# Attention scores from pairs of float16 products, with the softmax sums moved between engines

## The chip, the cores and the metric

The kernel runs on one core of one Trainium2 chip. The metric is the device time of one execution in microseconds (us). A core has TensorE (PE, matrix products), VectorE (DVE), ScalarE (ACT), GpSimd (POOL) and SyncE (SP, which here only issues transfers); each engine runs its own list of instructions in order, and waits for the others by semaphores.

## What is computed

Soft-capped attention (2 batches, 12 heads, 448 positions, head size 64) is followed by two feed-forward layers (768 to 2048 to 768, ReLU squared, then SiLU) over 896 tokens.

```python
def _attn_ref(q, k, v, cap) -> np.ndarray:
    scale = 1.0 / np.sqrt(q.shape[-1])
    scores = scale * np.matmul(q, k.transpose(0, 1, 3, 2))
    scores = cap * np.tanh(scores / cap)
    scores = scores - np.max(scores, axis=-1, keepdims=True)
    attn = np.exp(scores)
    attn = attn / (np.sum(attn, axis=-1, keepdims=True) + 1e-09)
    return np.matmul(attn, v).astype(np.float32)
...
    x = _moe_ref(x=x, **moe_kwargs)      # relu(x @ w_in) ** 2 @ w_out
    return _moe2_ref(x=x, **moe2_kwargs) # silu(x @ w_in) @ w_out
```

Inputs and output are float32.

## The kernel before

The 24 heads (of both batches) are 12 pairs; a pair fills the 128 partitions of one `qk` tile with the 64 rows of q (and of k) of two heads. Two pairs, `A` and `B`, make a "quad" m = 0 to 5. The 448 keys of a pair are three pieces of 128 (`A0`, `A1`, `A2`, `B0`, ...) and a rest of 64; the rests of both pairs share one block, `C`. So a quad has seven blocks in the order A0 A1 A2 C B0 B1 B2, and all six quads have 42.

`attention_bounded` walks over them in 21 groups of two blocks; h counts the groups. What is emitted in pass h, in this order, is what each engine then runs in order:

- `scores` (L636 on): TensorE multiplies k by q in float32 into one of two score tiles in PSUM, one product per head (two for `C`, one for each pair); ScalarE takes the tanh of it into an `e` tile (8 of them). A/B products use 64 rows by 128 columns of the array, `C` products 64 by 64.
- ScalarE takes the exp of both blocks (L746), in place. So ScalarE's list is tanh, tanh, exp, exp for each group.
- loads: `pr.load` puts the q and k of the next quad's pairs on SP's queue (L581, L582; six `qk` tiles), behind what is queued there already.
- VectorE copies finished attention sums `px` out of PSUM (L703), then `add` (L669 on; L675, L677) adds up the exponentials of each pair's blocks into `total`, the rest block `C` too (L681).
- `values` (L652 on): TensorE multiplies v by the exponentials of the group before.
- At a quad's end `add_up` (L683 on) sums `total` over its partitions with TensorE (four float32 products with ones); `evacuate_sums` (L705 on) copies the result with VectorE to `sm`, and SP gathers it to `st`; a pass later `invert` (L712 on) takes reciprocals on VectorE and SP writes them to `scratch` in memory, and then SP fetches them back, spread over partitions, as `rb`. `normalise` multiplies with them.
- `ws.load_to` and `ws.step` slip the first feed-forward weights in: loads on SP, and between passes 5 and 16 twelve steps, eight of them VectorE's (lines L367, L395 and L220: `u_0f`, `hl_0f` and so on).

Elsewhere a float32 weight or activation is handled as a high and a low float16 part, and a product of two such pairs as three float16 products (`ORDER`: high by high, high by low, low by high). The feed-forward layers (line L934) already work so; the attention before does not. `Watch` collects the sums of the low parts (`low_part`, L215 on) and decides at the end whether a general path must run instead.

After the last pass, TensorE sums the last pair's exponentials (`sump`, L698) and goes on to the first feed-forward products (`ha_0f`).

Of the kernel before, what the change touches and what calls it, by code (L numbers as in the profile page):

```python
# [26 lines left out]
def softcap_attention_relu2_silu(  # L27
# [26 lines left out]
    WT = KT * 128  # L54
    HALF = KT // 2 * 128
    NHR = 2
    AHEAD = 6
    NR = 7
    BENT = 1
# [5 lines left out]

    POWER = {"x0": 16, "a": 13, "b": 14, "ga": 22, "x1": 23, "c": 13, "d": 14, "gc": 24}
    LOWS, SAMPLES = 256, KT + 10
    LEAST = 256.0 * 128 * S  # L70
    ONE = 2.0 ** -POWER["x0"]
# [8 lines left out]
    def bank(name):  # L80
        return psum.tile([128, 512], F32, tag="p", bufs=4, name=name)
# [11 lines left out]

    cap = cap.rearrange("(a b) -> a b", a=1)
    capt = const.tile([128, 1], F32, tag="capt", name="capt")
    cap1 = const.tile([1, 2], F32, tag="cap1", name="cap1")
    nc.scalar.dma_start(cap1[:, :1], cap)
    nc.gpsimd.dma_start(capt, cap.to_broadcast([128, 1]))

# [12 lines left out]
    def tile_of(w, t):  # L112
        at = 2 + t * 128 * WT * 8
        return w.bitcast(I8)[at : at + 128 * WT * 8].rearrange("(p n) -> p n", p=128)

    COL2 = 0.1892
    PROD, UNIT = 9 * COL2, 12 * COL2
    PLAIN = (("a", 0), ("a", 2))
# [453 lines left out]
    class Pairs:  # L572
# [1 line left out]


        def __init__(self, pool, tag):
            self.pool, self.tag, self.qk, self.vt, self.vc = pool, tag, {}, {}, {}

        def load(self, i):
            t = self.pool.tile([128, 2, S], F32, tag="qk", bufs=6, name=f"qk{i}{self.tag}")  # L580
            nc.sync.dma_start(t[:, 0], q[i])  # L581
            nc.sync.dma_start(t[:, 1], k[i])  # L582
            self.qk[i] = t

        def load_v(self, i):
            m, b = divmod(i, 2)
# [15 lines left out]
    def attention_bounded(att, spool, ws, x0):  # L602
# [15 lines left out]
        nc.vector.reciprocal(cap1[:, 1:], cap1[:, :1])  # L618
        nc.vector.tensor_scalar(cap1[:, 1:], cap1[:, 1:], SCALE, None, op0=ALU.mult)
        scale_s, scale_c = nc.scalar.alloc_register("scale_s"), nc.scalar.alloc_register("scale_c")  # L620
        nc.scalar.reg_load(scale_s, cap1[:, 1:].bitcast(I32))
# [5 lines left out]
        NQ = NP2 // 2  # L627
        blocks = [(m, x) for m in range(NQ) for x in ("A0", "A1", "A2", "C", "B0", "B1", "B2")]

        def pair_of(m, x):  # L630
            return 2 * m + "AB".index(x[0])

        def head(j):
            return slice(64 * j, 64 * j + 64)

        def scores(m, x):  # L636
            sp = bank2(spool, f"s{m}_{x}")
            for j in range(2):
                for b in range(2) if x == "C" else (None,):
                    qk = pr.qk[pair_of(m, x) if b is None else 2 * m + b]  # L640
                    c = 3 if b is not None else int(x[1])
                    nc.tensor.matmul(  # L642
                        sp[:, j, :S] if b is None else sp[head(b), j, :S],
                        lhsT=qk[head(j), 1, 128 * c : min(128 * c + 128, S)],
                        rhs=qk[head(j), 0],
                        start=True,
                        stop=True,
                    )
            t = ex[m, x] = att.tile([128, 2, S], F32, tag="e", bufs=8, name=f"e{m}_{x}")
            nc.scalar.activation(t, sp[:, :, :S], AF.Tanh, scale=scale_s)  # L650

        def values(m, x):  # L652
            for i in (2 * m, 2 * m + 1) if x == "C" else (pair_of(m, x),):
                if i not in px:
                    px[i] = bank(f"px{i}")
            e = ex[m, x]
            for b in range(2) if x == "C" else (None,):
                for j in range(2):
                    i = pair_of(m, x) if b is None else 2 * m + b
                    v_m = pr.vt[i]  # L660
                    nc.tensor.matmul(  # L661
                        px[i][head(j), :S],
                        lhsT=v_m[:, 3 * j + int(x[1])] if b is None else pr.vc[m][head(b), j],
                        rhs=e[:, j] if b is None else e[head(b), j],
                        start=x == "A0" or b == 1,
                        stop=x == "B2" or b == 0,
                    )

        def add(m, x):  # L669
            e, i = ex[m, x], None if x == "C" else pair_of(m, x)  # L670
            if i == NP2 - 1:
                return
            if x in ("A1", "B1"):
                t = total[i] = att.tile([128, 2, S], F32, tag=f"total{x[0]}", bufs=2, name=f"total{i}")
                nc.vector.tensor_tensor(t, ex[m, x[0] + "0"], e, op=ALU.add)  # L675
            if x in ("A2", "B2"):
                nc.vector.tensor_tensor(total[i], total[i], e, op=ALU.add)  # L677
            if x in ("C", "B1"):
                b = int(x == "B1")
                t = total[2 * m + b][head(b)]  # L680
                nc.vector.tensor_tensor(t, t, ex[m, "C"][head(b)], op=ALU.add)  # L681

        def add_up(m):  # L683

            s = sums[m] = bank(f"sum{m}")
            for b in range(2):
                for j in range(2):
                    at = 32 * (2 * b + j)
                    nc.tensor.matmul(  # L689
                        s[at : at + 32, :S], lhsT=one[:, :32], rhs=total[2 * m + b][:, j], start=True, stop=True  # L690
                    )

        def add_up_pair(i, t, start=True, stop=True, part=slice(0, 128)):
# [44 lines left out]
        todo, last = [], 2 * NQ - 2  # L738
# [124 lines left out]


    NEXT = {"a": "b", "c": "d"}
    ORDER = ((0, 0), (0, 1), (1, 0))

    def at(x):

# [861 lines left out]
```

## Time and profile before

| | before |
|---|---|
| median of 2 runs | 491.35 us (491.1 to 491.6) |
| profiled execution, its own time | 491.04 us |
| its span, first to last instruction | 489.1 us |
| TensorE busy | 481.5 us (98%) |
| VectorE busy | 433.2 us (89%) |
| ScalarE busy | 383.5 us (78%) |
| GpSimd busy | 33.2 us (7%) |
| granted TensorE clock | 0.998 |

The attention takes the first 87 us of the span and the feed-forward layers the rest. A line of a timeline gives the start and the length in us, engine, source line, operation, tiles (buffer numbers left out) and, in brackets, how long the engine had idled and for whom. In the chain of the work that ended last each piece stands with its start and length. "x8" counts records; a float32 product leaves two of them.

### The profile page before, as it was taken

The page shows a single profiled execution, that of the slowest core. Times are in us where ns is not written, and L with a number is a line of the kernel's source. Part 1 is how long each engine was busy: PE and PEld are TensorE (multiplying, and loading weights), DVE is VectorE, ACT ScalarE, POOL GpSimd, SP SyncE. Part 2 cuts the span into 40 slices and gives each one's busy share as a digit, 9 for nine tenths or more (in the row PEclk, how much of TensorE's full clock was granted, in tenths as well). Part 3 has the DMA queues.
Part 4 walks back from the last instruction along what each step waited for, and adds up shares of the span by engine and source line. Part 5 has one row for each costly group of instructions (what it writes and reads, how often), then busy time and mean ns, then how long its engine had stood idle before and what let it go on. Part 6 is the DMA issues. An engine that isn't in the chain of part 4 may idle for free.

```text
span 489.1 us, 7199 instructions
## 1 busy us (share of the span) xinstructions
PE 481.5 (98%) x2554; PEld 232.7 (48%) x2554; DVE 433.2 (89%) x810; ACT 383.5 (78%) x625; POOL 33.2 (7%) x35
## 2 busy tenths in 40 slices
PE   8999999999999999999999999999999999999995
PEld 4323333455555555555555555555555555545552
DVE  0779998997899999988799999999878999999983
ACT  5999996899989944999988879989868688792100
POOL 1001555300000000000000000000000000000000
PEclk9999999999999999999999999999999999999999
DMA  7847461243645123335573443222577953129024
GB/s 248 283 136 187 163 198 40 82 142 127 216 158 187 49 81 129 131 129 194 193 259 116 144 146 113 72 84 103 183 260 242 314 228 86 45 85 365 2 77 157
DMA packets 25843, 75.28 MB, mean 154 GB/s; under 512 B 3270, under 2 KB 17606, under 8 KB 25798
## 3 DMA queue, kind: packets, MB, share of 16 engines
q1 hardware_dynamic: 25620, 74.50, 45.9%
q8 instruction: 22, 0.36, 0.3%
q10 hardware_dynamic: 146, 0.23, 0.1%
q14 instruction: 23, 0.19, 0.1%
q0 software_dynamic: 32, 0.00, 0.0%
HBM read 66.39 MB, written 8.29 MB: 153 GB/s over the span
## 4 chain that ended last, share of the span: by engine, by line
PE 86%; DVE 9%; DMA 1%; issue 1%; ACT 1%; DVEq 0%; ACTq 0%
PE px L661 7%; PE p_6df L934 4%; PE p_4df L934 4%; PE p_0df L934 4%; PE p_2bf L934 4%; PE s_B L642 3%; PE s_A L642 3%; PE ha_0f L934 3%; PE yb_3f L934 3%; PE yb_0f L934 3%; PE yb_5f L934 3%; PE yb_4f L934 3%; PE yb_2f L934 3%; PE ha_1f L934 3%; PE yb_1f L934 3%; PE p_2df L934 2%
## 5 line engine op out<-in xcount | busy, mean ns | idle before, releaser
L650 ACT ACTIVATE e_A<-s_A 128x896 f32<-128x896 f32 x18 | 15.9, 919 | 4.1 <-PE s_A L642 3.9
L650 ACT ACTIVATE e_B<-s_B 128x896 f32<-128x896 f32 x18 | 15.9, 917 | 4.0 <-PE s_B L642 3.7
L746 ACT ACTIVATE e_A<-e_A 128x896 f32<-128x896 f32 x18 | 16.5, 955 | 0.0
L746 ACT ACTIVATE e_B<-e_B 128x896 f32<-128x896 f32 x18 | 16.5, 953 | 0.0
L1459 DVE SCALAR_TENSOR_TENSOR yf<-p_6df,yf 128x448 f32<-128x448 f32 x15 | 9.2, 623 | 5.1 <-PE p_6df L934 5.1
L681 DVE TENSOR_TENSOR total<-total,e_C 64x896 f32<-64x896 f32 x11 | 12.9, 1174 | 0.4
L884 DVE TENSOR_TENSOR yaf<-p_2bf,yaf 128x448 f32<-128x448 f32 x15 | 9.3, 621 | 0.7 <-PE p_2bf L934 0.5
L362 POOL CAST zerosf<-raw_wb_7f 128x768 f16<-128x768 bf16 x1 | 1.1, 1055 | 127.0 <-DVE u_33f L367 127.0
L1459 DVE SCALAR_TENSOR_TENSOR yf<-p_4df,yf 128x448 f32<-128x448 f32 x15 | 9.2, 620 | 0.3 <-PE p_4df L934 0.2
L677 DVE TENSOR_TENSOR total<-total,e_A 128x896 f32<-128x896 f32 x6 | 8.2, 1359 | 0.3
L220 DVE SCALAR_TENSOR_TENSOR x1f<-yaf,x1f 128x448 f16<-128x448 f32 x12 | 7.4, 619 | 0.8 <-ACT x1f L873 0.8
L675 DVE TENSOR_TENSOR total<-e_A,e_A 128x896 f32<-128x896 f32 x6 | 6.8, 1130 | 1.1 <-ACT e_A L746 1.1
L884 DVE TENSOR_TENSOR yaf<-yaf 128x448 f32<-128x448 f32 x12 | 7.3, 620 | 0.1
L873 ACT ACTIVATE x1f<-yaf 128x448 f16<-128x448 f32 x12 | 6.7, 565 | 0.1
L675 DVE TENSOR_TENSOR total<-e_B,e_B 128x896 f32<-128x896 f32 x5 | 6.5, 1294 | 0.0
L759 DVE TENSOR_SCALAR gcap<-gcap 128x1 f32<-128x1 f32 x1 | 0.2, 154 | 6.8 <-ACT gcap L758 6.8
L364 ACT ACTIVATE zerosf<-raw_wa13f 128x768 f16<-128x768 bf16 x1 | 1.1, 1072 | 6.5 <-DVE u_24f L367 6.5
L734 DVE RECIPROCAL r<-r 128x448 f32<-128x448 f32 x2 | 5.9, 2953 | 0.1
L249 ACT ACTIVATE junk<-x0f 128x896 bf16<-128x896 f16 x6 | 5.7, 944 | 0.2
L677 DVE TENSOR_TENSOR total<-total,e_B 128x896 f32<-128x896 f32 x5 | 5.5, 1091 | 0.4
L746 ACT ACTIVATE e_C<-e_C 128x896 f32<-128x896 f32 x6 | 5.7, 954 | 0.0
L707 DVE COPY sm<-sum 128x448 f32<-128x448 f32 x5 | 3.1, 624 | 2.8 <-PE sum L689 2.8
(1860 smaller groups left out, 1671.1 us busy)
## 6 DMA issues: line engine op xcount, KB each, us to landing
yf<-spill SPq DMA_DIRECT2D x12, 224.0 KB, 4.7
out<-yf SPq DMA_DIRECT2D x11, 224.0 KB, 2.2
rb<-scratch SPq DMA_DIRECT2D x10, 224.0 KB, 4.1
raw_wb_0f<-in_moe_w_out SPq DMA_DIRECT2D x2, 768.0 KB, 6.3
raw_wb_1f<-in_moe_w_out SPq DMA_DIRECT2D x2, 768.0 KB, 4.3
raw_wb_2f<-in_moe_w_out SPq DMA_DIRECT2D x2, 768.0 KB
raw_wb_3f<-in_moe_w_out SPq DMA_DIRECT2D x2, 768.0 KB, 4.3
raw_wb_4f<-in_moe_w_out SPq DMA_DIRECT2D x2, 768.0 KB, 4.2
```

Of the source, the lines that this page charges most:

```text
L220: nc.vector.scalar_tensor_tensor(lo, x, scale, hi, op0=ALU.mult, op1=ALU.subtract, accum_out=watch.low() if see else None)
L642: nc.tensor.matmul(sp[:, j, :S] if b is None else sp[head(b), j, :S], lhsT=qk[head(j), 1, 128 * c : min(128 * c + 128, S)], rhs=qk[head(j) ...
L650: nc.scalar.activation(t, sp[:, :, :S], AF.Tanh, scale=scale_s)
L661: nc.tensor.matmul(px[i][head(j), :S], lhsT=v_m[:, 3 * j + int(x[1])] if b is None else pr.vc[m][head(b), j], rhs=e[:, j] if b is None els ...
L675: nc.vector.tensor_tensor(t, ex[m, x[0] + "0"], e, op=ALU.add)
L677: nc.vector.tensor_tensor(total[i], total[i], e, op=ALU.add)
L681: nc.vector.tensor_tensor(t, t, ex[m, "C"][head(b)], op=ALU.add)
L746: nc.scalar.activation(ex[m, x], ex[m, x], AF.Exp, scale=scale_c)
L873: return Step("A", cols, lambda: nc.scalar.activation(at(out), at(src), func, scale=scale), list(deps))
L884: return Step(eng, cols, lambda: e.tensor_tensor(at(out), at(x), at(y), op=op), list(deps))
L934: nc.tensor.matmul(acc, lhsT=w(e_w, kk), rhs=x(e_x, kk), start=first and i == 0, stop=last and i == len(n) - 1, skip_group_check=more,)
L1459: st = Step("D", S + 8 * see, lambda: nc.vector.scalar_tensor_tensor(yb, acc, to_y, yb, op0=ALU.mult, op1=ALU.add, accum_out=watch.low() i ...
```

## The change

From the fifth block on, the scores are made of three float16 products instead of one float32 product. For this, a new function `split` has VectorE make, for each of the pairs 1 to 11, a high float16 part (scaled by 2 to the 8th) and a low one, with a watched sum, of the pair's whole `qk` tile (128 by 896). `split` of an A pair is emitted at the head of the pass two groups ahead of the pair's first block, in front of that pass's copies and additions; that of a B pair likewise ahead of `C`. The first four blocks stay float32. There are four `qk` tiles instead of six, and three of the new `qh` tiles. The tanh reads a scale without, and from the fifth block on with, the factor of the two scalings.

The rest block `C` is no longer added by VectorE (but for the last quad): its sum over partitions is four more float32 products with ones over 64 rows, emitted behind `values` of `C`; `add_up` later adds into the same PSUM tile, which is held for that long. ScalarE instead of VectorE copies this sum to `sm` (one `sm` tile instead of two).

```diff
         def split(self, i, watch):
+            t = self.hl[i] = self.pool.tile([128, 2, 2, S], F16, tag="qh", bufs=NQH, name=f"qh{i}{self.tag}")
+            scale, x = 2.0 ** POWER["q"], self.qk[i]
+            nc.vector.tensor_scalar(t[:, 0], x, scale, 1.0, op0=ALU.mult, op1=ALU.mult)
+            low_part(watch, t[:, 1], x, t[:, 0], scale)
...
-            for j in range(2):
-                for b in range(2) if x == "C" else (None,):
-                    qk = pr.qk[pair_of(m, x) if b is None else 2 * m + b]
-                    c = 3 if b is not None else int(x[1])
-                    nc.tensor.matmul(
-                        sp[:, j, :S] if b is None else sp[head(b), j, :S],
-                        lhsT=qk[head(j), 1, 128 * c : min(128 * c + 128, S)],
-                        rhs=qk[head(j), 0],
...
+            for ek, eq in ((None, None),) if whole else ORDER:
+                for j in range(2):
+                    for b in range(2) if x == "C" else (None,):
+                        i = pair_of(m, x) if b is None else 2 * m + b
+                        kt, qt = (pr.qk[i][:, 1], pr.qk[i][:, 0]) if whole else (pr.hl[i][:, ek, 1], pr.hl[i][:, eq, 0])
+                        nc.tensor.matmul(
+                            sp[:, j, :S] if b is None else sp[head(b), j, :S],
+                            lhsT=kt[head(j), keys],
+                            rhs=qt[head(j)],
+                            start=whole or (ek, eq) == ORDER[0],
+                            stop=whole or (ek, eq) == ORDER[-1],
+                        )
...
+            if x == "C" and m < NQ - 1:
+                sums[m] = bank(f"sum{m}")
+                for b in range(2):
+                    for j in range(2):
+                        at = 32 * (2 * b + j)
+                        nc.tensor.matmul(
+                            sums[m][at : at + 32, :S], lhsT=one[head(b), :32], rhs=e[head(b), j], start=True, stop=False
+                        )
...
-            if x in ("C", "B1"):
-                b = int(x == "B1")
+            if x == "C" and m == NQ - 1:
+                b = 0
...
-            t = att.tile([128, S], F32, tag="sm", bufs=2, name=f"sm{m}")
-            nc.vector.tensor_copy(t, sums.pop(m)[:, :S])
+            t = att.tile([128, S], F32, tag="sm", bufs=1, name=f"sm{m}")
+            nc.scalar.activation(t, sums.pop(m)[:, :S], AF.Copy)
...
         for h in range(len(groups) + 1):
+            for m, x in blocks[2 * h + SOON : 2 * h + SOON + 2] if h else blocks[: SOON + 2]:
+                i = 2 * m if x == "A0" else 2 * m + 1 if x == ("C" if m else "B0") else 0
+                if i:
+                    pr.split(i, ws.watch)
```

On VectorE, around the fourth quad's start (passes 11 to 13), the list before is this; `x_c` are finished attention rows, `st` the sums to be inverted, `hl` and `u` weights.

```order
L677 TENSOR_TENSOR total_460<-total_460,e_B_446 128x896
L726 TENSOR_TENSOR x_c1f<-x_c1f,rb_372 128x448
L703 COPY x_c5f<-px_430 128x448
L675 TENSOR_TENSOR total_518<-e_A_451,e_A_474 128x896
L677 TENSOR_TENSOR total_518<-total_518,e_A_479 128x896
L707 COPY sm_530<-sum_525 128x448
L726 TENSOR_TENSOR x_c2f<-x_c2f,rb_467 128x448
L367 SCALAR_TENSOR_TENSOR u_2f<-raw_wa2f,zeros 128x768
L681 TENSOR_TENSOR total_518<-total_518,e_C 64x896
L713 TENSOR_SCALAR st_532<-st_532,gcap 32x56
```

And at the same place now, from the inversion of the second quad's sums on:

```order
L735 RECIPROCAL st_496<-st_496 32x56
L397 TENSOR_SCALAR hl_0f<-u_0f 128x768
L591 TENSOR_SCALAR qh7f<-qk7f 128x896
L222 SCALAR_TENSOR_TENSOR qh7f,lows<-qk7f,qh7f 128x896
L724 COPY x_c4f<-px_485 128x448
L697 TENSOR_TENSOR total_571<-e_B_507,e_B_516 128x896
L222 SCALAR_TENSOR_TENSOR hl_0f,lows<-u_0f,hl_0f 128x768
L699 TENSOR_TENSOR total_571<-total_571,e_B_553 128x896
L747 TENSOR_TENSOR x_c1f<-x_c1f,rb_446 128x448
L591 TENSOR_SCALAR qh8f<-qk8f 128x896
L222 SCALAR_TENSOR_TENSOR qh8f,lows<-qk8f,qh8f 128x896
L724 COPY x_c5f<-px_525 128x448
```

The addition of `C` and the copy to `sm` are gone from VectorE's list, and the two instructions of each `split` stand in it, ahead of the pass's copy and additions.

SP's queue stands in the same order before and now. Around the loads of pair 8 it reads as follows; `scratch<-st` waits for the inversion on VectorE, and everything below it waits with it.

```order
L736 DMA scratch<-st_496 32x56
L597 DMA vt8f<-in_v 128x384
L601 DMA vc4f<-in_v 128x128
L742 DMA rb_577<-scratch 64x2x448 x2
L583 DMA qk8f<-in_q 128x448
L584 DMA qk8f<-in_k 128x448
L297 DMA raw_wb_0f<-in_moe_w_out 128x6144
L583 DMA qk9f<-in_q 128x448
L584 DMA qk9f<-in_k 128x448
```

Nothing moved in it; what moved is that VectorE now waits for these loads itself, two groups ahead of the scores.

On ScalarE, at the end of the second quad's sums (pass 8), the list is now:

```order
L664 ACTIVATE e_A_460<-s_A_453 128x896
L664 ACTIVATE e_C<-s_C 128x896
L771 ACTIVATE e_A_460<-e_A_460 128x896
L771 ACTIVATE e_C<-e_C 128x896
L728 ACTIVATE sm_494<-sum_397 128x448
L664 ACTIVATE e_B_507<-s_B_500 128x896
```

The fifth row is new and stands between two groups; there are five such rows, one for each quad but the last. Behind the attention the order of every engine's instructions is unchanged.

## Rows read from the trace of the kernel before

**Rows 1.** The page, part 1: busy time, share, instructions of each engine.

```profile
PE 481.5 (98%) x2554; PEld 232.7 (48%) x2554; DVE 433.2 (89%) x810; ACT 383.5 (78%) x625; POOL 33.2 (7%) x35
```

**Rows 2.** Chain that ended last, in order of time: start us, us, what.

```profile
33.84 0.91 PE s_C L642 x8
...
76.98 0.89 PE sum L689 x8
77.88 1.70 PE s_B L642 x8
...
81.39 2.55 PE sump L698 x12
...
86.95 4.65 PE ha_0f L934 x24
```

**Rows 3.** Timeline of ScalarE: start us, us, line, operation, [idle before].

```profile
13.24 0.22 ACT L757 ACTIVATE gcap<-gcap 128x1 f32<-128x1 f32 x1
...
38.30 1.73 ACT L650 ACTIVATE e_B<-s_B 128x896 f32<-128x896 f32 x2 [0.88 <-PE s_B L642]
...
78.87 1.73 ACT L650 ACTIVATE e_B<-s_B 128x896 f32<-128x896 f32 x2 [0.90 <-PE s_B L642]
...
85.50 0.54 ACT L795 ACTIVATE x_c11f<-px 128x448 f32<-128x448 f32 x1 [3.22 <-PE px L661]
```

**Rows 4.** Busy us (instructions) by stretch: PE, PEld, DVE, ACT, POOL, clock, DMA share, GB/s.

```profile
23.42:67.75 44.33, 44.33 (x252) 13.83 (x252) 39.81 (x51) 40.99 (x50) 15.05 (x11) 1.00 0.58 169
...
29.46:55.39 25.93, 25.93 (x146) 8.01 (x144) 23.76 (x30) 23.88 (x29) 9.13 (x8) 1.00 0.68 205
```

**Rows 5.** Waits of TensorE over the whole span: us in total, times, longest.

```profile
PE ac14f L934 <- DVE s5c14f L884: 0.6, 1, 0.6
```

**Rows 6.** Timeline of TensorE in one block of rests, float32.

```profile
33.77 0.59 PE L642 MATMUL s_C<-qk4f 64*64 64x448 f32 x1
...
33.79 0.59 PE L642 MATMUL s_C<-qk4f 64*64 64x448 f32 x1
```

**Rows 7.** VectorE by line and shape, 5 to 87 us: busy us, mean ns, idle before.

```profile
L681 DVE TENSOR_TENSOR total<-total,e_C 64x896 f32<-64x896 f32 x11 | 12.9, 1174 | 0.4
...
L707 DVE COPY sm<-sum 128x448 f32<-128x448 f32 x5 | 3.1, 624 | 2.8 <-PE sum L689 2.8
```

**Rows 8.** Timeline of VectorE.

```profile
22.75 1.09 DVE L675 TENSOR_TENSOR total<-e_A,e_A 128x896 f32<-128x896 f32 x1 [1.08 <-ACT e_A L746]
...
42.20 0.48 DVE L395 TENSOR_SCALAR hl_0f<-u_0f 128x768 f16<-128x768 f32 x1
...
42.61 0.60 DVE L703 COPY x_c4f<-px 128x448 f32<-128x448 f32 x1
...
45.68 0.96 DVE L220 SCALAR_TENSOR_TENSOR hl_0f<-u_0f,hl_0f 128x768 f16<-128x768 f32 x1
...
46.56 1.09 DVE L677 TENSOR_TENSOR total<-total,e_B 128x896 f32<-128x896 f32 x1
...
69.69 0.60 DVE L703 COPY x_c8f<-px 128x448 f32<-128x448 f32 x1
```

**Rows 9.** Timeline of SP's queue: start us and us of each issue.

```profile
7.22 0.33 SPq L582 DMA_DIRECT2D qk2f<-in_k  x1
...
42.29 0.33 SPq L715 DMA_DIRECT2D scratch<-st  x1
...
45.70 0.43 SPq L582 DMA_DIRECT2D qk8f<-in_k  x1
...
56.89 0.33 SPq L715 DMA_DIRECT2D scratch<-st  x1
...
58.67 0.43 SPq L582 DMA_DIRECT2D qk10f<-in_k  x1
```

**Rows 10.** Transfers by tile: KB each, median us from issue to landing.

```profile
qk9f<-in_k SPq DMA_DIRECT2D x1, 224.0 KB, 6.5
qk10f<-in_k SPq DMA_DIRECT2D x1, 224.0 KB, 4.0
```

More of the change, by code (lines that the diff above doesn't have):

```diff
@@ L56, in softcap_attention_relu2_silu @@
     NHR = 2
+    NQK, NQH = 4, 3
     AHEAD = 6
@@ L61, in softcap_attention_relu2_silu @@
     SCALE = 1.0 / float(D) ** 0.5
-    POWER = {"x0": 16, "a": 13, "b": 14, "ga": 22, "x1": 23, "c": 13, "d": 14, "gc": 24}
+    POWER = {"q": 8, "x0": 16, "a": 13, "b": 14, "ga": 22, "x1": 23, "c": 13, "d": 14, "gc": 24}
     LOWS, SAMPLES = 256, KT + 10
@@ L95, in softcap_attention_relu2_silu @@
     capt = const.tile([128, 1], F32, tag="capt", name="capt")
-    cap1 = const.tile([1, 2], F32, tag="cap1", name="cap1")
+    cap1 = const.tile([1, 3], F32, tag="cap1", name="cap1")
     nc.scalar.dma_start(cap1[:, :1], cap)
@@ L114, in tile_of @@
         return w.bitcast(I8)[at : at + 128 * WT * 8].rearrange("(p n) -> p n", p=128)
+    ORDER = ((0, 0), (0, 1), (1, 0))
     COL2 = 0.1892
@@ L576, in __init__ @@
         def __init__(self, pool, tag):
-            self.pool, self.tag, self.qk, self.vt, self.vc = pool, tag, {}, {}, {}
+            self.pool, self.tag, self.qk, self.vt, self.vc, self.hl = pool, tag, {}, {}, {}, {}
         def load(self, i):
-            t = self.pool.tile([128, 2, S], F32, tag="qk", bufs=6, name=f"qk{i}{self.tag}")
+            t = self.pool.tile([128, 2, S], F32, tag="qk", bufs=NQK, name=f"qk{i}{self.tag}")
             nc.sync.dma_start(t[:, 0], q[i])
@@ L583, in load, with split @@
             self.qk[i] = t
+        def split(self, i, watch):
+            t = self.hl[i] = self.pool.tile([128, 2, 2, S], F16, tag="qh", bufs=NQH, name=f"qh{i}{self.tag}")
+            scale, x = 2.0 ** POWER["q"], self.qk[i]
+            nc.vector.tensor_scalar(t[:, 0], x, scale, 1.0, op0=ALU.mult, op1=ALU.mult)
+            low_part(watch, t[:, 1], x, t[:, 0], scale)
         def load_v(self, i):
@@ L617, in attention_bounded @@
         nc.vector.tensor_scalar(cap1[:, :1], cap1[:, :1], -CAP_MAX, CAP_MAX, op0=ALU.max, op1=ALU.min)
[L618 to L621, printed above, removed]
+        nc.vector.reciprocal(cap1[:, 1:2], cap1[:, :1])
+        nc.vector.tensor_scalar(cap1[:, 1:2], cap1[:, 1:2], SCALE, None, op0=ALU.mult)
+        nc.vector.tensor_scalar(cap1[:, 2:], cap1[:, 1:2], 2.0 ** (-2 * POWER["q"]), None, op0=ALU.mult)
+        scale_w, scale_s, scale_c = (nc.scalar.alloc_register(f"scale_{e}") for e in "wsc")
+        nc.scalar.reg_load(scale_w, cap1[:, 1:2].bitcast(I32))
+        nc.scalar.reg_load(scale_s, cap1[:, 2:].bitcast(I32))
         nc.scalar.reg_load(scale_c, cap1[:, :1].bitcast(I32))
@@ L625, in attention_bounded @@
         ex, total, px, sums, st, rb = {}, {}, {}, {}, {}, {}
-        NQ = NP2 // 2
+        NQ, WHOLE = NP2 // 2, 4
         blocks = [(m, x) for m in range(NQ) for x in ("A0", "A1", "A2", "C", "B0", "B1", "B2")]
@@ L637, in scores @@
             sp = bank2(spool, f"s{m}_{x}")
-            for j in range(2):
-                for b in range(2) if x == "C" else (None,):
-                    qk = pr.qk[pair_of(m, x) if b is None else 2 * m + b]
-                    c = 3 if b is not None else int(x[1])
-                    nc.tensor.matmul(
-                        sp[:, j, :S] if b is None else sp[head(b), j, :S],
-                        lhsT=qk[head(j), 1, 128 * c : min(128 * c + 128, S)],
-                        rhs=qk[head(j), 0],
-                        start=True,
-                        stop=True,
-                    )
+            c = 3 if x == "C" else int(x[1])
+            keys, whole = slice(128 * c, min(128 * c + 128, S)), (m, x) in blocks[:WHOLE]
+            for ek, eq in ((None, None),) if whole else ORDER:
[10 more added lines that the diff above has]
+                        )
             t = ex[m, x] = att.tile([128, 2, S], F32, tag="e", bufs=8, name=f"e{m}_{x}")
-            nc.scalar.activation(t, sp[:, :, :S], AF.Tanh, scale=scale_s)
+            nc.scalar.activation(t, sp[:, :, :S], AF.Tanh, scale=scale_w if whole else scale_s)
         def values(m, x):
@@ L683, in add_up @@
         def add_up(m):
-            s = sums[m] = bank(f"sum{m}")
             for b in range(2):
@@ L689, in add_up @@
                     nc.tensor.matmul(
-                        s[at : at + 32, :S], lhsT=one[:, :32], rhs=total[2 * m + b][:, j], start=True, stop=True
+                        sums[m][at : at + 32, :S], lhsT=one[:, :32], rhs=total[2 * m + b][:, j], start=False, stop=True
                     )
@@ L736, in last_sums @@
             return [a, b, c]
-        todo, last = [], 2 * NQ - 2
+        todo, last, SOON = [], 2 * NQ - 2, 4
         loads = {0: 0, 2: 1, 4: 2, 7: 3, 11: 4, 16: 5}
@@ L865, in softcap_attention_relu2_silu @@
     NEXT = {"a": "b", "c": "d"}
-    ORDER = ((0, 0), (0, 1), (1, 0))
     def at(x):
```

## The prediction

> **What bounds the kernel now.** I read the busy times first: TensorE is busy for 98% of the span, VectorE for 89%, ScalarE for 78% [rows 1]. That says little about the attention, so I went to the chain that ended last. From the first scores on it is TensorE almost without a break; its pieces in the attention are scores (0.85 a block: 1.70 for two), values, and 0.89 for a quad's sums, and at 86.95 the feed-forward products begin [rows 2]. Behind that, TensorE waits once, for 0.6 us [rows 5], and the change leaves the order there as it was. So whatever moves the point 86.95 moves the end by as much, and the question is what sets that point.
>
> In the attention the other engines are close behind. ScalarE's only real waits are 0.9 us for scores, once in each quad from the second on, where TensorE has done the sums first [rows 3]. In passes 5 to 16 (23.42 to 67.75, 12 groups in 44.33 us) ScalarE is busy for 40.99, 3.42 a group, and VectorE for 39.81 [rows 4]. VectorE's passes don't end where ScalarE's do: 1.7 us of pass 5 were done before 23.42 (an addition of 1.09 at 22.75 and a copy of 0.6), and pass 17 began on it only at 69.69, 2.0 us after ScalarE's [rows 8]. So its work in passes 5 to 16 is 39.8 + 1.7 + 2.0 = 43.5 us, hardly less than the 44.33 that they take. Three engines are within 8% of each other; a gain on one of them is worth what the next one leaves.
>
> **TensorE.** One block now costs three pairs of float16 products for two float32 ones. No float16 product over half the rows stands in the trace. What stands there: products on different parts of the array run side by side in float32 (two records of one tile start 0.02 us apart and eight records take 0.91 us in all [rows 2, 6]), and a float16 product over all rows takes 4.65/24 = 0.19 [rows 2]. Side by side a block costs 3 x 0.19 = 0.58; one after the other 6 x 0.19 = 1.16, and a block of rests 2.3. I take 0.65, near the lower end, since row halves are what overlapped before. That is 0.2 a block, 38 blocks, 7.6 us less; the five new sums of rests cost 0.89 each like the sums of today [rows 2], 4.5 us more. Net 3 us less, and less before each score, so ScalarE's 0.9 us waits go.
>
> The new sums have one form that no row shows: two row halves write one PSUM tile. The Trainium skill (TensorEngine Tiling (Array Packing), Restrictions and Gotchas) says that different row tiles cannot access the same PSUM bank at once. If so the two halves take turns; that is a rival below. No row of before shows such a pair.
>
> **ScalarE.** It gains five copies; the nearest row is its copy of the same shape, 0.54 [rows 3]. Four lie in passes 5 to 16: 41.0 + 4 x 0.54 = 43.2 us against 44.33. That alone allows a gain of 1.1 us there.
>
> **VectorE.** A split is one scaling, 0.48 for 768 columns, so 0.56 for 896, and one subtraction with a sum, 0.96 for 768, so 1.1 [rows 8]: 1.67 a pair. An addition of `C` that goes cost 1.17, a copy to `sm` 0.62 [rows 7]. Passes 5 to 16 hold seven splits, seven such additions and four copies: + 11.7 - 8.2 - 2.5 = + 1.0 us.
>
> The larger price is a wait. VectorE runs in order, and a split now waits for its pair's loads, at the head of a pass. For pair 8: the load of k was issued 3.4 us after the write of the inverted sums (42.29 to 45.70 [rows 9]), which itself waits for VectorE; a load lands 4.0 to 6.5 us after its issue [rows 10], say 5. So the pair is there about 8.4 us after VectorE's inversion. Between the inversion and the split of pair 8 VectorE has, by the new order, half a weight's split (0.48), the split of pair 7 (1.67), a copy (0.6), an addition (1.1), the other half (0.96), an addition (1.1) and a normalisation (0.6): 6.5 us [rows 8]. It waits 1.9 (0.9 to 3.4). Being late does not shorten that, since the load is released by VectorE's own inversion. For pair 10 the queue's part is 1.8 (56.89 to 58.67 [rows 9]) and the landing 4.0 [rows 10], 5.8 against 4.7 of work: 1.1. For pair 6 likewise 5.8 against the copy, two additions and one weight (3.8): 2.0. Together 5.0 us, and 49.5 us of VectorE for passes 5 to 16.
>
> Not all of it shows. VectorE starts pass 5 about 1.5 us ahead of ScalarE, and may end pass 16 behind: the split is done two groups ahead, the `total` of a quad is wanted by `add_up` a group and a half later. I take 2.5 us as what it may be late before `add_up`, and behind it the new copy on ScalarE, is held. So passes 5 to 16 take 49.5 - 1.5 - 2.5 = 45.5 us, 1.2 more than now.
>
> **The two ends.** At the start, the split of pair 2 stands ahead of VectorE's `gcap`, for which ScalarE waits at 13.24 [rows 3]. The load of k was issued at 7.22 [rows 9]: landed at 12.2 (11.2 to 13.7), split at 13.9, so ScalarE is 0.7 late (0 to 2.2). In passes 17 to 19 there are no weights left for VectorE, and ScalarE sets the pace: 3 x 3.42 + 0.54 = 10.8 where 11.1 were (67.75 to 78.87 [rows 3, 4]): 0.3 less. From the last group's first tanh (78.87) to the feed-forward (86.95) 8.1 us pass now. TensorE then has two blocks of values (0.83 each), three sums (2.55 [rows 2]), two more values and two sums (1.50); it reaches the three sums 0.5 + 0.8 earlier with cheaper scores, and the least is 6.0: ready for the sums at 0.3, done with them at 2.9, values at 4.5, sums at 6.0. VectorE, still about 2 us late with the last pair's `total`, holds it: I take 7.3, 0.8 less than now.
>
> **Sum.** + 0.7 + 1.2 - 0.3 - 0.8 = + 0.8 us on the profiled execution's own 491.04 us (span 489.1): 491.8. The median of the runs is 491.35, 0.3 above that execution, which is within their spread.
>
> **Rivals.** (1) *ScalarE sets the pace.* If loads land in 4 us and VectorE's lateness never reaches the others, passes 5 to 16 take 43.2 (- 1.1), the tail 6.0 (- 2.1), and the start and passes 17 to 19 as above: 491.0 + 0.7 - 1.1 - 0.3 - 2.1 = 488.2, and 487.5 without the start. For it: ScalarE waits for nothing but scores today. Against it: 43.5 us of VectorE's work in 44.33.
>
> (2) *Loads later still.* With 6.5 us a landing and all three waits at 1.5 us more, passes 5 to 16 take 50.0: 496.3. For it: SP's queue is held by the write of the sums, and now VectorE is held by the queue.
>
> (3) *The halves don't run side by side* (the other side). The place is `scores`. One after the other a block costs 1.16 for 0.85 (33 blocks, + 10.2), a block of rests 2.33 for 0.91 (5, + 7.1), with the sums + 4.5: TensorE, the bound, has 21.8 us more, 512.8. It decides from 0.28 a pair on; below that a block is no dearer than today. Against it: products on different parts of the array overlap today [rows 6].
>
> (4) *The two row halves of the new sums take turns.* Then a sum of rests costs 1.8. TensorE has in 3.5 groups 7 x (0.65 + 0.83) + 0.89 + 1.8 = 13.0 us, as much as the half of 25.93 that it has now [rows 4]: TensorE stays the bound, passes 5 to 19 take what they take now, the tail 7.3, and with the start it is 490.9. By the skill's rule above it would go so.
>
> **Chances.** The forecast, VectorE setting the pace, 0.50, with its own range 489.0 to 494.5 (the landing from 4.0 to 6.5 in one of three waits, the allowed lateness from 3.5 to 1). (1) 0.24. (2) 0.12. (3) 0.06. (4) 0.08. Leaving out the far ends of (1), the end of (2), and (3), 487.0 to 496.5 holds 8 in 10. A measurement of this kernel can tell about 2%, 9.8 us, from no change. Only (3) is over that: slower 0.07, with 0.01 for what I have not seen; faster 0.01, since ScalarE's own list leaves 4 us at most; within 2% 0.92.
>
> **What would show it.** VectorE should idle in front of the splits of pairs 6, 8 and 10, 1 to 3 us each, waiting for transfers, and start passes 14 to 17 some 3 us later than now against ScalarE. A score block should take 0.58 to 0.7 us and ScalarE's waits for scores behind the sums vanish. `ha_0f` should start at 87 to 88 us. The forecast is wrong if VectorE never waits for a `qk` load (then it is (1)), if ScalarE's copy or the sums wait by more than 1 us a quad (then lateness costs more), or if TensorE stays without gaps in passes 5 to 16 (then (3) or (4)).

## The result, and the profile after the change

| | before | after |
|---|---|---|
| median of 2 runs | 491.35 us | 496.65 us (496.32 to 496.99) |
| ratio to before | | 1.0116 (95%: 1.0100 to 1.0132) |
| profiled execution, its own time / span | 491.04 / 489.1 us | 496.99 / 495.2 us |
| TensorE, VectorE, ScalarE busy | 481.5, 433.2, 383.5 us | 481.2, 439.0, 384.4 us |
| first `ha_0f`, by TensorE's timeline | 86.89 us | 91.38 us |

The changed kernel is 1.2% slower, 4.85 us above the forecast and just above its range. The forecast's mechanism is there (VectorE sets the pace and waits for the `qk` loads), but it costs 5.3 us where less than 1 was forecast.

Where the time went is read off ScalarE, whose first tanh of a pass marks the passes. Its timeline after (the numbers in brackets: idle before, and for whom):

```profile
23.75 0.95 ACT L664 ACTIVATE e_C<-s_C 128x896 f32<-128x896 f32 x1
...
41.22 0.92 ACT L664 ACTIVATE e_B<-s_B 128x896 f32<-128x896 f32 x1
...
59.45 1.96 ACT L664 ACTIVATE e_A<-s_A 128x896 f32<-128x896 f32 x2 [4.21 <-PE s_A L656]
...
73.33 0.92 ACT L664 ACTIVATE e_B<-s_B 128x896 f32<-128x896 f32 x1 [2.39 <-PE s_B L656]
...
83.59 1.77 ACT L664 ACTIVATE e_B<-s_B 128x896 f32<-128x896 f32 x2
```

These are the starts of passes 5, 10, 14, 17 and 20. Before, pass 5 starts at 23.42 [rows 4], pass 10 at 41.82 and pass 17 at 67.75 [rows 4], pass 20 at 78.87 [rows 3]; the row of pass 10 is this:

```profile
41.82 0.92 ACT L650 ACTIVATE e_B<-s_B 128x896 f32<-128x896 f32 x1
```

So passes 5 to 9 gain 0.9 us (17.47 for 18.40), passes 10 to 16 lose 6.2 (32.11 for 25.93), passes 17 to 19 gain 0.9 (10.26 for 11.12), and the tail to `ha_0f` gains 0.2. At `ha_0f` the profiled execution is 4.5 us late, at the end of its span 6.1 (the medians differ by 5.3). The waits of VectorE in its passes 5 to 16 (which end where the split of pair 11 begins; us in total, times, longest):

```profile
DVE qh8f L591 <- PE px L675: 2.7, 1, 2.7
DVE qh6f L591 <- DMA qk6f<-in_k: 2.7, 1, 2.7
DVE st L734 <- DMA st<-sm: 2.3, 1, 2.3
DVE qh10f L591 <- DMA qk10f<-in_k: 1.0, 1, 1.0
DVE x_c0f L747 <- DMA rb<-scratch: 0.4, 1, 0.4
```

The first is named after `px`, but the split reads only `qk8f`; its load of k was issued at 48.09, 4.3 us behind the write of the inverted sums, and the split began at 53.36, 5.3 us later. In e6 below the trace puts the wait of the same split down to the load, 5.4 us behind its issue. And TensorE, which had no wait in these passes before, stands still twice, each time for a copy of `px` that VectorE runs behind a split (columns as in the ScalarE timeline):

```profile
55.71 0.96 PE L687 MATMUL sum<-e_C,ones 64*32 64x448 f32 x8 [2.43 <-DVE x_c5f L724]
...
71.66 0.96 PE L687 MATMUL sum<-e_C,ones 64*32 64x448 f32 x8 [1.78 <-DVE x_c7f L724]
```

The sum of the rests needs a PSUM bank that this copy frees. The granted clock fell behind the first of these gaps and not behind the second (by stretch; the sixth group of numbers is the clock):

```profile
56.00:58.00 2.00, 2.00 (x12) 0.20 (x4) 1.90 (x3) 0.00 (x0) 0.00 (x0) 0.71 0.02 8
58.00:60.00 2.00, 2.00 (x14) 0.72 (x12) 2.00 (x3) 0.55 (x1) 1.44 (x2) 0.50 0.00 0
60.00:62.00 2.00, 2.00 (x12) 0.48 (x8) 1.97 (x4) 1.87 (x3) 1.05 (x1) 0.94 0.00 0
```

### The profile page after: what moved, and what is told of

The parts are those of the page before. It is cut to its first block, busy times and chain, and to the rows that moved or that the text cites. A ratio compares the mean times of both kernels' runs of the same rounds, so it can differ in the third digit from the quotient of the medians.

```text
span 495.2 us, 7471 instructions
## 1 busy us (share of the span) xinstructions
PE 481.2 (97%) x2680; PEld 231.2 (47%) x2680; DVE 439.0 (89%) x829; ACT 384.4 (78%) x630; POOL 30.3 (6%) x35
## 4 chain that ended last, share of the span: by engine, by line
PE 75%; DVE 13%; DMA 6%; ACT 2%; issue 2%; SPq 0%; DVEq 0%; ACTq 0%
PE p_6df L958 4%; PE p_2bf L958 4%; PE p_0df L958 4%; PE p_4df L958 4%; PE px L675 4%; PE p_2df L958 3%; PE yb_2f L958 3%; PE yb_4f L958 3%; PE yb_0f L958 3%; PE yb_3f L958 3%; PE yb_5f L958 3%; PE yb_1f L958 3%; PE ha_1f L958 2%; DMA raw_wd_5f<-in_moe_w_out 1%; PE ac0f L958 1%
## 5 line engine op out<-in xcount | busy, mean ns | idle before, releaser
L687 PE MATMUL sum<-e_C,ones 64*32 64x448 f32 x40 | 4.8, 548 | 4.2 <-DVE x_c5f L724 2.4
L699 DVE TENSOR_TENSOR total<-total,e_A 128x896 f32<-128x896 f32 x6 | 7.2, 1200 | 0.5
L710 PE MATMUL sum<-total,ones 128*32 128x448 f32 x40 | 6.2, 551 | 0.0
```

The source lines that it names most:

```text
L710: nc.tensor.matmul(sums[m][at : at + 32, :S], lhsT=one[:, :32], rhs=total[2 * m + b][:, j], start=False, stop=True)
```

## The experiments

From this trace came **theory 1**: the late copy and the bank held from `C` on are the loss, with the clock's fall to 1.2 GHz on top; early loads or copies ahead of the splits cure it. **Theory 2** is wider: VectorE as a whole is the pace, what it works or waits longer is paid, and the bank is only the first thing that is late. The rival to both: the moved sums and copies are the cost. All ratios are to the kernel before on the same chip.

| kernel | median us | ratio (95%) | first `ha_0f` |
|---|---|---|---|
| after the change | 496.65 | 1.0116 (1.0100 to 1.0132) | 91.38 |
| e1 loads two passes earlier | 492.86 | 1.0040 (1.0025 to 1.0056) | 87.03 |
| e2 splits behind copies and additions | 493.97 | 1.0056 (1.0041 to 1.0072) | 88.90 |
| e3 float16 scores only | 503.16 | 1.0266 (1.0237 to 1.0295) | 98.12 |
| e4 sums and copies only | 495.24 | 1.0085 (1.0072 to 1.0098) | 91.53 |
| e5 e1 and e2 | 491.44 | 0.9999 (0.9982 to 1.0015) | 87.77 |
| e6 bank taken two passes later | 496.60 | 1.0119 (1.0098 to 1.0140) | 90.46 |
| e7 e1, six `px` copies by ScalarE | 489.05 | 0.9977 (0.9962 to 0.9993) | 84.64 |
| e8 six `px` copies by ScalarE | 494.10 | 1.0059 (1.0037 to 1.0080) | 90.46 |
| e9 loads later | 507.76 | 1.0343 (1.0325 to 1.0362) | 102.86 |
| e10 e1, first inversion later | 494.48 | 1.0079 (1.0066 to 1.0092) | 89.07 |
| e11 before, six copies by ScalarE | 491.19 | 1.0006 (0.9997 to 1.0014) | 86.89 |
| e12 e1, weights' steps earlier | 496.21 | 1.0100 (1.0082 to 1.0119) | 87.19 |
| e13 e7 and e12 | 495.89 | 1.0092 (1.0075 to 1.0108) | 86.93 |
| e14 e1, no subtraction on GpSimd | 487.98 | 0.9941 (0.9927 to 0.9954) | 83.35 |
| e15 before, no subtraction on GpSimd | 490.96 | 0.9998 (0.9989 to 1.0007) | 87.30 |

**e1: the loads earlier.**

```diff
+                for m, x in sum(groups[h + 2 : h + 3] if h else groups[:3], []):
                     if x in ("A1", "C") and m + 1 < NQ:
                         pr.load(2 * m + 2 + (x == "C"))
```

> The loads of each later pair's q and k are emitted two passes earlier on SP's queue, ahead of the transfers that wait for VectorE's inversion; nothing else changes. Theory (late splits make the copies of px late, and the sum tile that is now held from C on needs the freed PSUM bank): VectorE's waits of 2.7, 2.7 and 1.0 us before the splits of pairs 6, 8 and 10 vanish, TensorE's waits of 2.4 and 1.8 us at the sums vanish with them, the granted clock stays at 1.00 all through the attention, the first feed-forward product starts at 86 to 88 us instead of 91.4, and the time is 488 to 491.5 us. Rival (the splits' own work on VectorE, and the sums and copies moved to TensorE and ScalarE, are the cost): the waits for loads go but the time stays at 494 to 497.

492.86: 3.4 of the 5.3 us are back, the load waits are gone, the clock stays at 1.00. But the time lies between the two expectations. VectorE now waits for other things instead, 1.7 us for the first `rb` and 1.8 for `st`, and in passes 10 to 16 VectorE is still all but full (the fourth group of numbers is VectorE's busy time; here from the split of pair 7 to that of pair 11, 29.16 us; after the change it was 31.63):

```profile
42.25:71.41 29.16, 26.92 (x202) 7.77 (x200) 28.64 (x41) 25.54 (x33) 13.57 (x11) 1.00 0.56 167
```

```profile
44.12:75.75 31.63, 27.42 (x190) 7.59 (x188) 27.46 (x41) 24.17 (x30) 10.95 (x11) 0.95 0.54 168
```

**e2: copies and additions ahead of the splits** (the four lines of the split loop moved behind the `add` loop).

> The splits are emitted behind the copies and additions of their pass instead of ahead of them; the loads stay where they are. Theory: VectorE still waits for loads before splits 6, 8 and 10 (by some 1 us less each, since it comes later), but the px copies are done before, so TensorE no longer waits at the sums and its clock stays at 1.00; the time is 489 to 493 us. Rival (what costs is that VectorE is late as a whole, wherever the split stands): TensorE's waits at the sums become waits for the split pairs at the scores or for total, and the time stays at 495 to 497.

493.97, between the two expectations. TensorE no longer waits at the rests' sums. But VectorE's waits for loads also fell, from 6.3 to 1.0 us, since a split now asks only behind a copy and two additions. So this run does not separate the place of the copy from the waits.

**e3 and e4: one part alone.** In e3 the rests are added and the sums copied by VectorE as before; in e4 all scores are float32 (`WHOLE` 4 to 42), there are six `qk` tiles as before and no splits.

> Only the first part of the change: scores as three float16 products; the rests are added by VectorE and the sums copied by VectorE as before the change, and the sum tile is opened only where a quad ends. Theory: no sum tile asks for a bank behind a late px copy, so TensorE has no waits of more than 1 us at the sums for px; but VectorE has 5 additions of 1.17 and 5 copies of 0.62 us more and is the pace: 493 to 497. Rival (the new sums on TensorE and the copies on ScalarE are what costs): 488.5 to 491 us.

> Only the second part: the rests' sums by TensorE and their copies by ScalarE; all scores are float32 products as before the change and there are no splits, so VectorE never waits for a load. Theory: TensorE's five new sums of 0.89 us come on top of an attention in which it is the bound, VectorE has 8 us less and is never late, and no px copy is waited for: 493 to 496 us with the clock at 1.00. Rival (the tile held from C on is a loss by itself, VectorE late or not): TensorE waits over 1 us in a quad at the sums, and the time is over 497.

e4 came out as expected: TensorE has no gap, and `ha_0f` is 4.6 us later, about five sums of 0.89 (4.5). e3 came out 6 us above its range: there is no long-held bank in it, and it is the slowest of these four. From 44 to 84 us:

```profile
44.00:84.00 40.00, 31.01 (x210) 9.05 (x208) 39.31 (x55) 28.16 (x34) 15.36 (x12) 0.96 0.44 138
```

VectorE is busy for 39.3 of 40 us. So neither part pays alone: the splits overload VectorE, and the second part, which takes some 7 us off the result by relieving VectorE, costs 4.3 on TensorE where VectorE is not the pace.

**e5 and e6: both edits, and the bank alone.** e6 emits the rests' products two passes later, so that the bank is taken that much later:

```diff
-            if x == "C" and m < NQ - 1:
-                sums[m] = bank(f"sum{m}")
...
+            for m, x in groups[h - 3] if h > 2 else []:
+                if x == "C" and m < NQ - 1:
+                    rests(m)
```

> Both earlier edits at once: the loads of q and k two passes earlier, and the splits behind the copies and additions of their pass. Theory 1 (only the loads and the place of the copies matter): no wait for a load, no wait for a bank, 490 to 491.5 us. Theory 2 (behind them VectorE's own work of passes 9 to 17 is what is left, since with early loads it is busy for 9.8 of every 10 us from 44 to 84 us): the second edit adds nothing to the first, 492 to 494 us.

> The changed kernel with one thing moved: the rests' four products with ones, and with them the taking of the PSUM bank for the sum, come two passes later on TensorE. Loads, splits and copies stay. Theory 1 (the bank held from C on is the main loss): TensorE's waits of 2.4 and 1.8 us for px copies vanish, the clock stays at 1.00, and the time is 491.5 to 494 us. Theory 2 (VectorE is late as a whole, and the bank is only the first thing that is late): the waits for px vanish, others for split pairs or totals take their place, and the time is 494.5 to 497 us.

**e6 brings theory 1 down.** The waits for `px` are gone, and the time is what it was (496.60). Others came in their place, at the scores:

```profile
PE s_C L656 <- DVE qh9f L222: 1.5, 1, 1.5
PE s_C L656 <- DVE qh9f L591: 1.3, 1, 1.3
PE s_A L656 <- DVE qh8f L222: 0.8, 1, 0.8
PE s_C L656 <- DVE qh11f L222: 0.7, 1, 0.7
```

The granted clock was 1.00 throughout 54 to 64 us in e6, and that gained nothing either: VectorE was late, and TensorE at 1.2 GHz only waited less. e5 ends level with the kernel before. Its time lies in theory 1's range (490 to 491.5) and below theory 2's, so taken by itself it speaks for theory 1. But its `ha_0f` is no earlier than in e1 (87.77 and 87.03); so the second edit gained nothing in the attention, and what e5 gains lies behind: VectorE waits 1.1 us for the last `rb` in place of 2.8, and the 1.2 us for which e1's TensorE waits at `ha_1f` are gone.

**e7 and e8: VectorE relieved, with early loads and without.**

```diff
-            nc.vector.tensor_copy(cell(i), px.pop(i)[:, :S])
+            if i in (4, 5, 6, 7, 8, 9):
+                nc.scalar.activation(cell(i), px.pop(i)[:, :S], AF.Copy)
+            else:
+                nc.vector.tensor_copy(cell(i), px.pop(i)[:, :S])
```

> Loads two passes earlier, and the copies of px of pairs 4 to 9 by ScalarE instead of VectorE: VectorE has 6 x 0.61 = 3.7 us less between 44 and 84 us, ScalarE, which is idle for about 5 us there, has 6 x 0.54 = 3.2 us more. Theory 2 (VectorE's own work is what is left once the loads are early): 488.5 to 491 us, that is at or below the kernel before. Theory 3 (ScalarE is as much the bound): no gain over early loads alone, 492.5 to 495 us.

> Only the copies of px of pairs 4 to 9 go to ScalarE; the loads and the splits stay where the change put them. The copy no longer stands behind a split that waits for its load, so the bank for the sum is free in time. Theory 1: VectorE still waits 2 to 3 us before the splits of pairs 6 and 8, TensorE no longer waits for px, the clock stays at 1.00, and the time is 490 to 492.5 us. Theory 2 with the load waits as VectorE's largest loss: TensorE waits for split pairs or for totals instead, 493 to 496 us.

e7 is faster than the changed kernel, and than the kernel before by 0.23% (0.07 to 0.38), a small gain: its runs go from 488.4 to 491.7. 3.7 us of work off VectorE gave 3.8 us. ScalarE is then busy without a break from 24 to 74 us (fifth group of numbers):

```profile
24.00:74.00 50.00, 49.50 (x386) 14.56 (x384) 47.02 (x63) 50.00 (x67) 16.41 (x13) 1.00 0.53 162
```

That is the state of the prediction's rival 1, ScalarE as the pace. That its time is met too (488.2 forecast for it; the profiled execution of e7 took 488.45) is partly luck: passes 5 to 16 took 42.9 us, where the rival had 43.2, with eight copies on ScalarE where it counted four, because a group and a copy cost less than it took (3.28 and 0.42 us from start to start, for 3.42 and 0.54). In e8 the waits for loads stayed (3.7, 1.9 and 1.6 us), and so did 3.2 us of the loss, as theory 2 says.

**e9 to e11: more lateness, a third kind of wait, and the copies in the kernel before.** e9 puts the loads at the end of their pass; e10 is e1 with `h + 1 + (m == 0)` and `h + 2 + (m == 0)` for `invert` and `fetch`; e11 is e7's edit alone in the kernel before.

> The other direction: the loads of q and k of pairs 2 to 11 are emitted at the end of the pass at whose head they were emitted, behind that pass's fetch of rb and load of weights. VectorE's waits before the splits of pairs 6, 8 and 10 grow. Theory 2 (VectorE is the pace, and every wait at the head of a pass is paid by the attention): the waits together grow from 6.3 to 9 us or more, and the time to 499 to 504 us. Rival (most of the waiting for loads is hidden): 496 to 498 us.

> Early loads, and the inversion of the first quad's sums and the fetch of its rb one pass later, so that VectorE no longer waits for that quad's sums to land (1.8 us at about 29 us with early loads alone). If that wait counts like those for loads: 491 to 492 us, 1 to 2 below early loads alone. If it only holds VectorE where ScalarE sets the pace, up to 44 us: 492.5 to 494 us.

> The kernel before the change, with nothing but the copies of px of pairs 4 to 9 moved from VectorE to ScalarE. If moving these copies is a gain by itself, changed scores or not: 488.5 to 490 us. If it pays only where VectorE is late (theory 2): 491 to 493 us, since TensorE without a gap is the bound of the kernel before and ScalarE gets 3.2 us more.

In e9 VectorE waits 20.5 us for loads where it waited 6.3:

```profile
DVE qh6f L591 <- DMA qk6f<-in_k: 6.6, 1, 6.6
DVE qh5f L591 <- DMA qk5f<-in_k: 6.3, 1, 6.3
DVE qh8f L591 <- DMA qk8f<-in_k: 4.9, 1, 4.9
DVE qh10f L591 <- DMA qk10f<-in_k: 2.7, 1, 2.7
```

This is above the expected 499 to 504, as the waits are far over the 9 us that were expected at the least. VectorE's waits for `st` and `rb` are gone there, so that it waits 20.8 us in all, where the changed kernel had 9.0, and 11.8 us more of waiting cost 11.1. TensorE's granted clock was below 1.00 for part of that time too (0.66 from 70 to 80 us), so not all of it need be VectorE's. In e10 the wait for the first sums is gone, but `rb` comes later and VectorE waits 5.2 us for it, up to 42.6 us; the kernel loses 1.6 us against e1 and is above both expectations, so this run does not tell what the wait for the sums is worth, only that a wait of VectorE for `rb` counts too. e11 shows that moving the copies is no gain by itself: the ratio is 1.0006. It pays where VectorE is late.

**e12 and e13: the weights' steps two a pass in passes 5 to 9** (`ws.step(2 if h < 10 else 1)`).

> Early loads, and the steps of the first weights two a pass in passes 5 to 9 and one a pass behind. In passes 10 to 16 VectorE has 2.4 us less of them (1.85 instead of 4.2 us), in passes 5 to 9 as much more; no engine does more or less work in all. Theory 2, made narrower (VectorE has no time to spare in passes 10 to 16, where it is busy for 28.6 of 29.2 us with early loads, and has 3 to 4 us to spare before): 490 to 491.5 us. Rival (VectorE's work counts wherever it stands): 492.5 to 494 us, as with early loads alone.

> Early loads, copies of px of pairs 4 to 9 by ScalarE, and the weights' steps two a pass in passes 5 to 9. If ScalarE has become the pace with the copies (it was busy without a break from 24 to 74 us then), the moved steps add nothing: 488.5 to 489.5 us. If VectorE is still late somewhere: 487 to 488.5 us.

Both missed, and the edit did not do what was meant. Two steps in each of five passes and one in each of seven make 17 steps, where there were 12: five steps that stood behind the attention came into it as well, two of them VectorE's and three ScalarE's. VectorE's weights in passes 5 to 9 grew from 2.3 to 6.5 us, and behind fell only from 4.2 to 2.8. The split of pair 7 starts at 44.33 (42.25 in e1), which used up the relief behind; `ha_0f` stays (87.19 and 87.03), and e13's comes 2.3 us later than e7's. The rest of the loss is behind the attention, where three weight instructions now stand ahead of VectorE's subtraction for `x0f` of pair 10; in e1 they come later, and it starts at 92.38:

```profile
91.21 1.31 DVE L222 SCALAR_TENSOR_TENSOR hl_3f<-u_3f,hl_3f 128x768 f16<-128x768 f32 x1
...
92.45 1.78 DVE L369 SCALAR_TENSOR_TENSOR u_5f<-raw_wb_1f,zeros 128x768 int32<-128x768 int32 x1
94.16 1.30 DVE L222 SCALAR_TENSOR_TENSOR hl_4f<-u_4f,hl_4f 128x768 f16<-128x768 f32 x1
95.38 1.45 DVE L222 SCALAR_TENSOR_TENSOR x0f<-x_c10f,x0f 128x448 f16<-128x448 f32 x1
```

TensorE then waits for the two parts of pair 11, which come behind it:

```profile
PE ha_1f L959 <- ACT x0f L898: 2.5, 1, 2.5
PE ha_1f L959 <- DVE x0f L222: 1.0, 1, 1.0
```

So neither run tests the narrower theory, that only passes 10 to 16 are full: there is more work in the attention, and another order behind it.

**e14 and e15: GpSimd's work away.** VectorE's splits took very unequal times. The split of pair 9 after the change, and GpSimd at the same time:

```profile
59.17 0.98 DVE L591 TENSOR_SCALAR qh9f<-qk9f 128x896 f16<-128x896 f32 x1
60.19 1.80 DVE L222 SCALAR_TENSOR_TENSOR qh9f<-qk9f,qh9f 128x896 f16<-128x896 f32 x1
```

```profile
58.48 1.20 POOL L1581 TENSOR_SCALAR x0f<-x_c2f 128x448 f16<-128x448 f32 x1 [5.04 <-DVE x_c2f L747]
59.76 1.28 POOL L1582 TENSOR_TENSOR x0f<-x_c2f,x0f 128x448 f16<-128x448 f32 x1
```

and that of pair 8, with GpSimd idle but for its first 0.1 us (a cast ends there at 53.44):

```profile
53.36 0.63 DVE L591 TENSOR_SCALAR qh8f<-qk8f 128x896 f16<-128x896 f32 x1 [2.70 <-PE px L675]
54.02 1.09 DVE L222 SCALAR_TENSOR_TENSOR qh8f<-qk8f,qh8f 128x896 f16<-128x896 f32 x1
```

The normalisation by VectorE releases GpSimd's two instructions on the finished row, and VectorE's next instructions, in four passes a split among them, run into them. The edit:

```diff
-            nc.gpsimd.tensor_tensor(lo, r, hi.bitcast(F32) if self.dt == F32R else hi, op=ALU.subtract)
+            nc.gpsimd.memset(lo.bitcast(I32), 0)
```

> Early loads, and GpSimd's subtraction for the low part of each finished attention row of pairs 0 to 9 is replaced by writing zeros (that low part is left out of the result). In the traces VectorE's split of a pair takes up to 1.45 + 1.80 us instead of 0.62 + 1.09 where such a subtraction runs, and ends 0.5 or 0.9 us behind it. If VectorE waits there for GpSimd, and VectorE is the pace: the splits of pairs 7, 9, 10 and 11 come down by 2 to 3 us together, and the time falls from 492.9 to 489.5 to 491.5 us. If these delays are hidden: 492 to 494 us.

> The same replacement of GpSimd's subtraction by zeros in the kernel before the change, nothing else (the low part of the attention rows of pairs 0 to 9 is left out of the result). TensorE without a gap is the bound there, so a faster VectorE should bring nothing: 490.5 to 492 us. If GpSimd holds back that kernel too: below 490 us.

e14: 487.98, 4.9 us below e1 and more than expected; e15: no change. In e14 `ha_0f` comes 3.7 us earlier than in e1, and TensorE's wait of 1.2 us at `ha_1f` is gone. From the split of pair 7 to that of pair 11 VectorE now needs 26.24 us:

```profile
42.27:68.51 26.24, 26.17 (x200) 7.77 (x200) 25.72 (x40) 25.09 (x32) 9.18 (x10) 1.00 0.64 185
```

The hold-ups by GpSimd were there before the change and cost nothing, since TensorE was the bound. With VectorE as the pace they are part of the price. What they cost in the changed kernel itself, with its late loads, was not run. e14 leaves work out and is no version to use; e7 is.

## Why the prediction was wrong, by its own steps

- **What sets the pace: right.** VectorE does, it idles before the splits of pairs 6, 8 and 10, and the waits of ScalarE behind the sums that stood in each quad [rows 3] are gone; those that remain are VectorE's lateness. e1, e7, e8 and e9 all move with VectorE.
- **"49.5 us of VectorE for passes 5 to 16": the step that failed.** They took 54.7 (from the split of pair 4 at 21.05 to that of pair 11 at 75.75):

```profile
21.05:75.75 54.70, 50.39 (x372) 14.30 (x370) 44.84 (x67) 47.24 (x59) 12.84 (x13) 0.97 0.51 155
```

  Busy time was 44.8, where I had 44.5, so the sum of the work was good. The loads cost 6.3 us where I had 5.0: the queue's part before pair 8 was 4.3 for 3.4 and the landing about 5.3 for 5, and pair 6's came 6.7 us behind the write of the sums for 5.8. These make 1.3 us. The other 3.5 us were in no term: 2.3 for `st`, 0.4 for `rb`, and 0.9 of small gaps. I had summed busy time and added only the new waits, though the trace of before shows such waits too: 2.8 us before the copies to `sm` [rows 7].
- **"I take 2.5 us as what it may be late before `add_up` ... is held": right in size, wrong in place.** VectorE started pass 5 2.7 us ahead of ScalarE (1.5 allowed; before the change it was 2.4, with the copy of `x_c1f` at 21.06) and pass 17 2.4 us behind: 54.7 - 2.7 - 2.4 = 49.6 is what passes 5 to 16 took, for 45.5 forecast. What was held first was not `add_up` but the rests' sum, through its bank. In e6 this place is free in time and the kernel is as slow.
- **What the average hid.** I took VectorE's room from the whole of passes 5 to 16, 39.8 of 44.3 us [rows 4]. By halves, up to and from the start of VectorE's pass 10 at 42.61 (before the change; second number VectorE busy), it is:

```profile
22.15:42.61 20.46, 16.17 (x22) 1.00 0.52 152
42.61:69.69 27.08, 26.21 (x35) 1.00 0.64 196
```

  79% (78% from the copy at 21.06, with which VectorE's pass 5 begins) and 97%. In passes 10 to 16, where all of the loss is, there was nothing to take the 3.7 us of load waits and the delay of pair 6.
- **The splits' price.** 1.67 us a pair holds for four of the seven (0.63 and 1.09); pairs 7, 9 and 10 took 2.5 to 2.9 beside GpSimd. That is 3.1 us more than the three cost in the sum. It came out all the same, by luck, since other work took less than before, partly additions that GpSimd had held up: the second addition of an A pair took 1359 ns before and 1200 now. e14 shows what taking GpSimd's subtractions away is worth once VectorE is the pace and the loads are early, 4.9 us; the prediction did not have such a term.
- **The signs named.** VectorE idled before the splits of pairs 6, 8 and 10, 2.7, 2.7 and 1.0 us, as said. Against ScalarE its pass 14 was to start some 3 us later than before, and did: it begins with the copy of `x_c6f`, 3.6 us behind ScalarE's pass 14 (59.45) after the change, and 0.7 us behind it before. VectorE after, VectorE before, ScalarE before:

```profile
63.02 0.60 DVE L724 COPY x_c6f<-px 128x448 f32<-128x448 f32 x1
```

```profile
57.20 0.60 DVE L703 COPY x_c6f<-px 128x448 f32<-128x448 f32 x1
```

```profile
56.46 1.73 ACT L650 ACTIVATE e_A<-s_A 128x896 f32<-128x896 f32 x2
```

  By pass 17 it was only 0.5 more (2.4 for 1.9), since ScalarE had come to wait itself and was 5.6 us late. `ha_0f` came at 91.4, not at 87 to 88. One sign of being wrong, a wait of the sums by more than 1 us a quad, "then lateness costs more", came true twice (2.43 and 1.78 us).
- **TensorE: right.** A float16 score block takes 0.62 (0.65 forecast), and the rival with halves one after the other is out. The rests' sums took 0.96 like the others, so rival 4 is out as well:

```profile
82.24 1.31 PE L656 MATMUL s_B<-qh11f 64*128 64x448 f16 x12
```

```profile
L710 PE MATMUL sum<-total,ones 128*32 128x448 f32 x40 | 6.2, 551 | 0.0
L687 PE MATMUL sum<-e_C,ones 64*32 64x448 f32 x40 | 4.8, 548 | 4.2 <-DVE x_c5f L724 2.4 <-DVE x_c7f L724 1.8
```

- **The ends.** Start + 0.3 (+ 0.7 forecast), passes 17 to 19 - 0.9 (- 0.3; ScalarE's group and copy cost 3.28 and 0.42 us, where I had 3.42 and 0.54), tail - 0.2 (- 0.8). Behind the attention I had nothing and it was + 1.6: VectorE, late, inverts the last quad's sums late, waits 2.2 us for their `rb` at 95.0, and TensorE waits 0.55 for `x0f` and later 0.5 for `u2c10f`. The remaining 0.5 was not traced.
- **The chances.** Within 2% was right. The range stopped short because rival 2, loads later still, was worked out with the same VectorE budget; with 3.5 us of waits left out, every case of it sat too low.

Not settled: what the wait for the first quad's sums alone is worth (e10 brought another wait), and what the weights' steps cost in each half (e12 and e13 moved more of them than meant).

## What to carry to other kernels

When an engine that is 90% busy gets new work or new waits, look at its busy share stage by stage, and count the waits that it has today with its work: the stage at 97% has next to nothing to pay with. If the engine that is late stops another one, freeing that one place moves the stop; take waits or work off the late engine itself. And look at which engine an instruction of the late engine has just released: it may be the one that holds up its next instruction.

## What the runs showed of the hardware

- **VectorE waits for a whole GpSimd instruction.** GpSimd's two instructions end at 59.68 and 61.04; VectorE's two beside them end 0.47 and 0.95 us behind, at 60.15 and 61.99; in the splits of pairs 7 and 10 it is 0.47, 0.48 and 0.89. The Trainium skill (SBUF — State Buffer, Who interferes with whom) says that the two engines share a port pair, which an instruction of either holds to its end; VectorE's instructions with two inputs in SBUF need it, and some with one input; this trace agrees, and e14 (with early loads) and e15 give the price of GpSimd's subtractions: 4.9 us where VectorE is the pace, nothing where it isn't.
- **Two row halves may write one PSUM bank at full speed.** The rests' products from both halves of the rows into one tile took 548 ns a record and 0.96 us for eight, products over all rows 551 ns. The Trainium skill (TensorEngine Tiling (Array Packing), Restrictions and Gotchas) has it that different row tiles cannot access one bank at the same time; here the four products write different partitions of it, 32 each, and the measurement shows no turns being taken. No run here has two row halves on the same partitions.
- **One gap of TensorE was followed by the lower clock, another not.** Behind 2.43 us of waiting the granted clock was 0.71 and 0.50 in the next two stretches of 2 us, and four `px` products took 1.57 us for 0.92; behind 1.78 us it stayed at 1.00, and so it did in e6, with TensorE busy for 1.26 of 4 us from 58 to 62.
